# Attention and a top-1 expert layer on one core: score tiles in a ring for the first two quads, and the last quad's sums moved ahead of a group of scores

## The chip, the cores and the metric

The kernel runs on one core of one Trainium2 chip. Times are device microseconds (us) of one execution. The kernel before took 807.14 us in the median of three runs (805.10 to 809.29). TensorE (PE in the profile) multiplies matrices, ScalarE (ACT) evaluates functions, VectorE (DVE) does elementwise work, GpSimd (POOL) issues the gathers, scatters and some copies, and SyncE (SP) issues the loads. PE writes its results to PSUM, a memory of eight banks; a bank holds 512 fp32 numbers for each of the 128 partitions.

## The reference

The inputs are q, k and v of 8 batches, 12 heads, 448 positions and 64 features. The scores are capped with a tanh, and attention is followed by a layer of eight experts of which each token uses one:

```python
scores = q @ k.T / 8
scores = cap * tanh(scores / cap)
attn = exp(scores - max); attn = attn / (sum(attn) + 1e-9)
x = (attn @ v) with the heads side by side        # 3584 tokens x 768
logits = x @ w_gate + modality_bias[modality_id]  # 3584 x 8
e = argmax(logits); gate = softmax(logits)[e]
out = gate * (relu(x @ w1[e]) @ w2[e])            # 768 -> 1024 -> 768
```

## The kernel before

The heads are worked off in 24 **quads**, four heads of one batch each (three quads to a batch). Scores are kept transposed, with keys on partitions and queries along the row, so that the sums over keys are done by PE. The 448 keys of a head are three tiles of 128, and a rest of 64; the rests of the four heads share one tile ("shared", L529 to L537). The two pairs of heads of a quad are t = 0 and t = 1, and the three key tiles are i = 0, 1, 2.

A pass i of the loop at L801 has three parts r, whose operations stand in the list ORDER (L767 to L778), each with the quad that it works on, counted from i. Every engine runs its instructions in the order in which they are issued here. Part 0 makes the shared scores of quad i (`group` with the step None, L563 to L598) and adds the shared products with V of quad i-1 (`pvs`, L617). Part 1 makes the scores of t = 0, then the products with V of t = 1 of quad i-1 (`pv`, L606), copies them out of PSUM (`xs`, L640), and splits the next quad's operands into a rounded and a rest part (`split_hi`, `split_lo`). Part 2 makes the scores of t = 1, then the `sums` of quad i-1 (L648: the softmax denominators and the unscaled gate logits, 16 matmuls in one PSUM tile "glog"), then the products with V of t = 0 of quad i, the copy `gl` of glog (L660), denominators (`den`, L684) and others. In the first pass part 1 comes ahead of part 0, and in the parts (0, 2) and (1, 1) the products with V are issued between the second and the third score tile of the group.

`group` issues the scores of its tiles on PE and then, on ACT, a tanh for each tile and one exponential over all three. A score tile is 128 keys by two heads, two banks of PSUM. There are two pools: `score_tile(4)` gives a tile of four banks, which holds i = 0 and 1 of a group, and `score_tile(2)` gives one of two banks, which holds i = 2 and also the shared scores. In the groups of t = 1 one tanh covers the four banks (L588, L589); in those of t = 0 each tile has its own. The other two banks are xT0 and xT1 (L470 to L472): the accumulators of the products with V, and in between glog and small routing tiles, which take the name in `self.small`.

When a batch's three quads are done, `route` (L238 to L310) works out which expert each token takes and its rank among the expert's tokens: two small matmuls ("rank", L273 and L275), DVE work around them, and four indirect stores to a map in DRAM. It is a generator, of which `next(routing[0])` and STEPS issue a stretch in certain parts. For batch 6 these parts fall in the last pass with scores, i = 23 (= NQ - 1).

In part 2 of pass 23 four operations of the list are replaced (L811, L812): DVE scales the gathered rows of the first expert's tokens, and the turned logits of quad 22 (`lt`, L679) are written to a bank of the score tile. Pass 24 (the list LAST, L779 to L783) ends the last quad and turns the gathered rows on PE (L1054), and the expert stage begins: blocks of 384 tokens, with w1 and w2 of the block's expert loaded, split into two parts and multiplied in three products (L1124, L1125, L1128 and L1160).

Of the kernel before, what the change touches and what calls it, by code (L numbers as in the profile page):

```python
# [39 lines left out]
F32 = mybir.dt.float32  # L40
# [4 lines left out]
ALU = mybir.AluOpType  # L45
AX = mybir.AxisListType
PSUM = bass.MemoryType.PSUM
# [6 lines left out]
KU, KR = 3, 64  # L54
# [26 lines left out]
NQ = NH * B  # L81
# [5 lines left out]
class Program:  # L87
# [8 lines left out]
    def pin(self, inst):  # L96
        return self.tc.keep_in_program_order(inst)
# [365 lines left out]
    def attention(self, first, rp):  # L463
        tc, nc = self.tc, self.nc
        pe, pin = nc.tensor, self.pin
        with ExitStack() as st:
# [3 lines left out]
            ps_x = st.enter_context(tc.tile_pool(name="ps_x", bufs=1, space=PSUM))  # L470
            for t in range(2):
                ps_x.tile([128, 512], F32, name="xT", tag=f"xT{t}")  # L472
            ps_s = [st.enter_context(tc.tile_pool(name=f"ps_s{n}", bufs=1, space=PSUM)) for n in (4, 2)]
            self.ps_r = ps_x
            quads = [dict(live=i < NQ, kq={}, hl={}, pt={}, tot={}, xT={}, xs={}) for i in range(NQ + 1)]

# [46 lines left out]
                        self.scales()  # L523
                quads[0]["hl"][0] = hi, lo

            def score_tile(n):
                return ps_s[n == 2].tile([128, n, 512], F32, name="sc")

            def shared(q):  # L529
                sc = score_tile(2)  # L530
                for t in range(2):
                    for j in range(2):
                        kq, rows = quads[q]["kq"][t], slice(j * D, (j + 1) * D)
                        pin(pe.matmul(
                            sc[t * KR : (t + 1) * KR, j, :S], kq[rows, :KR], kq[rows, KC2:], start=True, stop=True
                        ))
                return sc  # L537

            def scores(q, t, i):
                if i == 0:  # L540
                    quads[q]["four"] = score_tile(4)
                sc = quads[q]["four"][:, 2 * i : 2 * i + 2] if i < 2 else score_tile(2)
                if q == t == i == 0:
                    kq = quads[q]["kq"][t]
                    for j in range(2):
                        rows = slice(j * D, (j + 1) * D)
                        pin(pe.matmul(sc[:, j, :S], kq[rows, KR : KR + 128], kq[rows, KC2:], start=True, stop=True))
                    return sc
                hi, lo = quads[q]["hl"][t]
                ks = slice(i * 128, (i + 1) * 128)  # L550
                for n, (k, x) in enumerate(((hi, hi), (hi, lo), (lo, hi))):
                    for j in range(2):
                        rows = slice(j * D, (j + 1) * D)
                        pin(pe.matmul(sc[:, j, :S], k[rows, ks], x[rows, OWN:], start=n == 0, stop=n == 2))  # L554
                return sc

            def tanh(out, sc, scale):
                pin(nc.scalar.activation(out, sc[:, :, :S], AF.Tanh, scale=scale))  # L558
# [4 lines left out]
            def group(q, steps, amid=None):  # L563

                if q >= NQ:
                    return
                d, made = quads[q], []
                for step in steps:
                    if (q, step) in FILL:
                        self.warm(self.ps_r, FILL[q, step])  # L570
                    if amid and step == steps[-1]:
                        amid()
                    made.append(scores(q, *step) if step else shared(q))
                if "sh" not in d:
                    d["both"] = pp.tile([128, KU + 1, 2, S], F32, name="pt0", bufs=2)
                    d["sh"] = d["both"][:, KU]
                if steps == (None,):
                    tanh(d["sh"], made[0], self.isc)
                    d["later"] = [d["sh"]]
                    if q == 0:  # L580
                        exp(d["later"].pop())
                    return
                t = steps[0][0]
                three = pp.tile([128, KU, 2, S], F32, name="pt1", bufs=1) if t else d["both"]
                scale = 1.0 if (q, t) in SCALED else self.isc
                for n in range(KU):
                    d["pt"][t, n] = three[:, n]
                if t:  # L588
                    tanh(three[:, :2].rearrange("p n j s -> p (n j) s"), d["four"], scale)  # L589
                for n in range(2 if t else 0, KU):  # L590
                    if amid and n == KU - 1 and d.get("later"):
                        exp(d["later"].pop())
                    tanh(three[:, n], made[n], scale)
                whole = three[:, :KU]
                if d.get("later"):
                    d["later"].pop()
                    whole = three
                exp(whole.rearrange("p n j s -> p (n j s)"))  # L598

            FILL = {(0, (1, 2)): 4}  # L600
            SCALED = [(q, t) for q in range(3) for t in range(2)][1:]

# [44 lines left out]

            def sums(q):  # L648
                d = quads[q]
                glog = d["glog"] = ps_x.tile([128, 512], F32, name="glog", tag="xT1" if q < NQ - 1 else "xT0")  # L650
                w = [self.wgt[:, 2 * (q % NH) + t] for t in range(2)]
                for n, four in enumerate((
                    ((0, d["tot"][0][:, 0]), (0, d["tot"][1][:, 0]), (0, d["tot"][0][:, 1]), (2, d["sh"][:, 0])),
                    ((w[0], d["xs"][0]), (w[1], d["xs"][1]), (1, d["tot"][1][:, 1]), (3, d["sh"][:, 1])),
                )):
                    for c, (what, rhs) in enumerate(four):
                        lhs = self.pick[:, what] if isinstance(what, int) else what
                        pin(pe.matmul(glog[c * GW : (c + 1) * GW, :S], lhs, rhs, start=n == 0, stop=n == 1))
# [25 lines left out]
            def den(q):  # L684
                l, gw = quads[q]["lt"], GC if q < NQ - 2 else GW
                b, r = divmod(q, NH)
                if r == 0:
                    lgs[b] = self.lp.tile([CP, C, H, E], F32, name="lg")
                    pays[b] = self.lp.tile([CP, C, MR], F32, name="pay", bufs=2)
                    nc.gpsimd.memset(pays[b][:, :, 2 + H :], 0.0)  # L690
                rec = pays[b][:, :, 2 : 2 + H].rearrange("p c (j k) -> p c j k", j=2)[:, :, :, 2 * r : 2 * r + 2]
                shared = l[:, :, 3 * gw + GE : 3 * gw + GE + 4].rearrange("p c (j t) -> p c j t", j=2)
                pin(nc.vector.tensor_copy(rec, shared))
                for j, own in enumerate((l[:, :, GE : GE + gw + 1 : gw], l[:, :, 2 * gw + GE : 2 * gw + GE + 2])):
                    pin(nc.vector.tensor_tensor(rec[:, :, j], own, rec[:, :, j], op=ALU.add))
                pin(nc.vector.reciprocal(rec, rec))
                for t in range(2):
                    h0 = 4 * r + 2 * t
                    pin(nc.vector.tensor_tensor(
                        lgs[b][:, :, h0 : h0 + 2], l[:, :, t * gw : t * gw + GE].rearrange("p c (j e) -> p c j e", j=2),  # L700
                        rec[:, :, :, t].unsqueeze(3).to_broadcast([CP, C, 2, E]), op=ALU.mult,
                    ))
# [89 lines left out]
            lgs, pays, routing, raws, banks, homes = {}, {}, [], [], [], []  # L792
# [7 lines left out]
            fetch_v(1)  # L800
            for i in range(NQ + 1):  # L801
                for r in (1, 0, 2) if i == 0 else range(3):
                    if (i, r) == (0, 1):
                        split_hi(0, 1)
                        split_lo(0, 1)
                    if (i, r) == (NQ, 0):
                        tot1(NQ - 1, 1)
                        tot2(NQ - 1, 1)
                        self.scale_rows(early[1], homes, (1,))
                    ops = list((ORDER if i < NQ else LAST)[r])  # L810
                    if (i, r) == (NQ - 1, 2):  # L811
                        ops[-4:] = (scale, 0), (lt, -1), (den, -1), ops[-2]  # L812
                    if (i, r) == (NQ - 1, 1):
                        ops.insert(ops.index((split_lo, 1, 0)), (lambda q: next(routing[0]), 0))
                    if (i, r) in ((0, 2), (1, 1)):
                        values = [op for op in ops if op[0] is pv]
                        ops = [op for op in ops if op[0] is not pv]
                        ops[0] += (lambda: [pv(i + n, *how) for _, n, *how in values],)
                    for op, n, *how in ops:
                        q = i + n  # L820
# [4 lines left out]
                    if r == 2:  # L825
                        fetch(i + 2, 1)
                        fetch_v(i + 2)
                    self.small = "xT0" if r == 1 and i else "xT1"
                    for _ in range(STEPS.count((i, r))):
                        next(routing[0], None)  # L830
                    if (i, r) in WAYS:
# [755 lines left out]
```

## Time and profile before

| | |
|---|---|
| median of three runs | 807.14 us (805.10 to 809.29) |
| profiled execution | 803.42 us, span 801.8 us, mean granted clock 0.997 |
| PE busy | 784.8 us (98% of the span), 5184 instructions |
| DVE busy | 556.0 us (69%) |
| ACT busy | 507.3 us (63%) |
| POOL busy | 306.6 us (38%) |

"Busy" is the time in which an engine's instructions run, and for PE the ends of matmuls are modelled. An instruction's idle time is what its engine stood still before it, with what ended that. A line of the profile names the kernel's line, the engine, the operation, and the tiles as out<-in. Attention and its passes reach from the start to about 318 us, and the expert stage from there to the end.

### The profile page before, as it was taken

What the parts mean: (1) busy time and instruction counts of PE and PEld (TensorE: products, weight loads), DVE (VectorE), ACT (ScalarE), POOL (GpSimd) and SP (SyncE); (2) the same over time, 40 slices, a digit from 0 to 9 for tenths busy, and PEclk for the clock granted to TensorE, in tenths of its full rate; (3) what the DMA queues carried; (4) which work ended last, traced back from release to release, by engine and by line L of the source; (5) the groups of instructions that cost most, each with busy time, mean ns of one, the idle gap of its engine ahead of it and who ended that gap; (6) DMA issues with size and microseconds to landing.
All of it is one profiled execution on the core that took longest, in us unless ns stands there. A gap on an engine that the chain in (4) does not pass through costs nothing. (4 is left out here: it accounts for less than half of the span.)

```text
span 801.8 us, 14472 instructions
## 1 busy us (share of the span) xinstructions
PE 784.8 (98%) x5184; PEld 613.9 (77%) x5184; DVE 556.0 (69%) x1085; ACT 507.3 (63%) x552; POOL 306.6 (38%) x382
## 2 busy tenths in 40 slices
PE   7999999999999989999999999999999999999997
PEld 3444544444444444999999999999999999999986
DVE  5889999999999997957284652747527375366820
ACT  7999999999999995256253452534526345245611
POOL 2122434232425162448555173551744407051201
PEclk9999999999999999999999999999999999999999
DMA  7477756767576663498357273563725627257654
GB/s 261 131 180 196 199 134 198 196 159 219 145 216 175 180 165 104 96 315 259 126 183 250 101 239 111 180 237 113 247 103 175 253 93 242 90 176 247 214 216 160
DMA packets 103808, 146.01 MB, mean 182 GB/s; under 512 B 62255, under 2 KB 67457, under 8 KB 103730
## 3 DMA queue, kind: packets, MB, share of 16 engines
q1 hardware_dynamic: 88832, 110.69, 46.2%
q0 software_dynamic: 14752, 34.33, 12.7%
q8 instruction: 43, 0.70, 0.4%
q14 instruction: 35, 0.29, 0.1%
q10 hardware_dynamic: 146, 0.00, 0.0%
HBM read 118.06 MB, written 27.49 MB: 182 GB/s over the span
## 5 line engine op out<-in xcount | busy, mean ns | idle before, releaser
L1124 PE MATMUL ph<-x,ah 128*128 128x384 f32 (+1 forms) x480 | 156.3, 326 | 1.0 <-DVE hl L1135 1.0
L1125 PE MATMUL ph<-x,ah 128*128 128x384 f32 (+1 forms) x480 | 155.9, 325 | 0.0
L1128 PE MATMUL ph<-x,al 128*128 128x384 f32 (+1 forms) x480 | 155.9, 325 | 0.0
L1160 PE MATMUL py<-bh,hh 128*128 128x384 f32 x448 | 150.3, 335 | 0.0
L1160 PE MATMUL py<-bh,hl 128*128 128x384 f32 x448 | 149.8, 334 | 0.0
L1160 PE MATMUL py<-bl,hh 128*128 128x384 f32 x448 | 146.5, 334 | 0.0
L558 ACT ACTIVATE pt<-sc,isc 128x896 f32<-128x896 f32 x132 | 140.2, 1118 | 7.5 <-PE sc L554 4.9
L561 ACT ACTIVATE pt<-pt,cabs 128x2688 f32<-128x2688 f32 (+2 forms) x50 | 140.6, 2811 | 1.6
L991 POOL DMA_INDIRECT xg<-xd,at x93 | 117.8, 1267 | 56.8 <-DVE turned L1077 30.0
L720 POOL DMA_DIRECT2D xd<-xs x96 | 61.1, 644 | 178.2 <-DVE xs L714 175.4
L1012 DVE TENSOR_TENSOR bl<-raw,bh 128x768 fp32r<-128x768 f32 x80 | 74.3, 956 | 70.7 <-ACT bh L1011 70.5
L612 PE MATMUL xT<-pt,va 128*64 128x448 f32 x576 | 118.8, 548 | 0.1
L1134 ACT ACTIVATE hh<-ph 128x384 fp32r<-128x384 f32 (+1 forms) x80 | 37.4, 469 | 126.6 <-PE ph L1128 121.4
L1135 DVE SCALAR_TENSOR_TENSOR hl<-ph,hh 128x384 fp32r<-128x384 f32 (+1 forms) x80 | 41.8, 527 | 105.7 <-ACT hh L1134 105.7
L1124 PEld LDWEIGHTS ph<-x,ah 128*128 128x128 f32 x480 | 90.2, 188 | 1.2 <-DVE hl L1135 1.2
L1125 PEld LDWEIGHTS ph<-x,ah 128*128 128x128 f32 x480 | 90.1, 188 | 0.0
L612 PEld LDWEIGHTS xT<-pt,va 128*64 128x64 f32 x576 | 37.0, 136 | 69.4 <-issue 56.0
L1128 PEld LDWEIGHTS ph<-x,al 128*128 128x128 f32 x480 | 90.1, 188 | 0.0
L1166 POOL DMA_INDIRECT out_dram<-ot,mt x28 | 32.1, 1146 | 146.5 <-ACT ot L1165 128.6
L1160 PEld LDWEIGHTS py<-bh,hh 128*128 128x128 f32 x448 | 84.1, 188 | 1.1 <-issue 0.7
L1160 PEld LDWEIGHTS py<-bh,hl 128*128 128x128 f32 x448 | 84.1, 188 | 0.1
L1160 PEld LDWEIGHTS py<-bl,hh 128*128 128x128 f32 x448 | 83.8, 188 | 0.0
(216 smaller groups left out, 1265.3 us busy)
## 6 DMA issues: line engine op xcount, KB each, us to landing
raw<-in_w_dram SPq DMA_DIRECT2D x86, 384.0 KB, 3.9
raw<-in_w_dram SPq DMA_DIRECT2D x60, 512.0 KB, 5.5
kq<-in_kq_dram SPq DMA_DIRECT2D x47, 448.0 KB, 5.9
va<-in_v_dram SPq DMA_DIRECT2D x24, 448.0 KB, 6.2
xd<-xs POOLq DMA_DIRECT2D x96, 112.0 KB, 5.2
lgd<-gl SPq DMA_DIRECT2D x88, 35.0 KB, 2.9
cg<-lgd SPq DMA_DIRECT2D x22, 140.0 KB, 5.6
raw<-in_w_dram SPq DMA_DIRECT2D x12, 256.0 KB, 5.5
```

Source lines behind the costliest of these rows:

```text
L558: pin(nc.scalar.activation(out, sc[:, :, :S], AF.Tanh, scale=scale))
L561: pin(nc.scalar.activation(x, x, AF.Exp, scale=self.cabs))
L612: pin(pe.matmul(xT[j * D : (j + 1) * D, :S], va[:, u * D : (u + 1) * D], quads[q]["pt"][t, i][:, j], start=t == i == 0, stop=t == 1 and i ...
L720: (nc.gpsimd.dma_start(self.xd[b * S : (b + 1) * S, a, r * 64 : (r + 1) * 64].rearrange("(n p) f -> p n f", p=32), d["out"][a * 32 : (a + ...
L991: got = self.nc.gpsimd.indirect_dma_start(self.xg[:, c], None, self.xd.rearrange("n a x -> (n a) x"), bass.IndirectOffsetOnAxis(ap=at[:, c ...
L1012: b = self.nc.vector.tensor_tensor(lo, raw, hi, op=ALU.subtract)
L1124: nc.tensor.matmul(ph[:, :w], hi[:, fs], self.x[k][:, 0, :w], start=first, stop=False)
L1125: nc.tensor.matmul(ph[:, :w], hi[:, fs], self.x[k][:, 1, :w], start=False, stop=False)
L1128: nc.tensor.matmul(ph[:, :w], lo[:, fs], self.x[k][:, 0, :w], start=False, stop=last)
L1134: nc.scalar.activation(hh[:, f, :w], acc, AF.Relu)
L1135: self.latest["vector"] = nc.vector.scalar_tensor_tensor(hl[:, f, :w], acc, 0.0, hh[:, f, :w], op0=ALU.max, op1=ALU.subtract).ins
L1160: self.latest["tensor"] = nc.tensor.matmul(py[half][:, :HALF], self.h[a][:, f, rows], self.w2s[f][c][:, cs], start=left[half] == 3 * FC - ...
```

## The change

Quads 0 and 1 (RING = 2) take their score tiles from three pools of two banks in turn, and each tile has a tanh of its own. At the start of part 0 of pass 2 the three pools are closed, and a pool of four banks and one of two are opened on the same six banks; from there on the score tiles are as before.

In pass 23 (NQ - 1) the sums and the copy gl of quad 22 are taken out of part 2 and put at the end of part 1, ahead of the second group of scores of quad 23. The routing step that stood in part 1 stays where it was, ahead of them, and the rank step of batch 6 (in STEPS) follows them. glog of quad 22 lies in xT0 now and the small tiles of this part in xT1. The name `eng` in `den` is VectorE, as before.

```diff
-            ps_s = [st.enter_context(tc.tile_pool(name=f"ps_s{n}", bufs=1, space=PSUM)) for n in (4, 2)]
+            ring = ExitStack()
+            score_pool = lambda home, name, **kw: home.enter_context(tc.tile_pool(name=name, bufs=1, space=PSUM, **kw))
+            ps_s = [score_pool(ring, f"ps_s{n}") for n in range(3)]
...
-            def score_tile(n):
+            def score_tile(n=2):
+                if len(ps_s) == 3:
+                    ps_s.append(ps_s.pop(0))
+                    return ps_s[-1].tile([128, n, 512], F32, name="sc")
                 return ps_s[n == 2].tile([128, n, 512], F32, name="sc")
 
+            def pairs():
+                ring.close()
+                ps_s[:] = [score_pool(st, f"ps_s{n}", reuse_waits="tile") for n in ("four", "two")]
...
-                if i == 0:
-                    quads[q]["four"] = score_tile(4)
-                sc = quads[q]["four"][:, 2 * i : 2 * i + 2] if i < 2 else score_tile(2)
+                if i == 0 and q >= RING:
+                    four[:] = [score_tile(4)]
+                sc = four[0][:, 2 * i : 2 * i + 2] if i < 2 and q >= RING else score_tile()
...
-                if t:
-                    tanh(three[:, :2].rearrange("p n j s -> p (n j) s"), d["four"], scale)
-                for n in range(2 if t else 0, KU):
+                joined = t and q >= RING
+                if joined:
+                    tanh(three[:, :2].rearrange("p n j s -> p (n j) s"), four[0], scale)
+                for n in range(2 if joined else 0, KU):
...
+            RING, four = 2, []
...
-                glog = d["glog"] = ps_x.tile([128, 512], F32, name="glog", tag="xT1" if q < NQ - 1 else "xT0")
+                glog = d["glog"] = ps_x.tile([128, 512], F32, name="glog", tag="xT1" if q < NQ - 2 else "xT0")
...
                 for r in (1, 0, 2) if i == 0 else range(3):
+                    if (i, r) == (RING, 0):
+                        pairs()
...
+                    if i == NQ - 1 and r:
+                        late = [(sums, -1), (gl, -1)]
+                        ops = [op for op in ops if op not in late] + (late if r == 1 else [])
...
                     if (i, r) == (NQ - 1, 1):
-                        ops.insert(ops.index((split_lo, 1, 0)), (lambda q: next(routing[0]), 0))
+                        ops.insert(ops.index((sums, -1)), (lambda q: next(routing[0]), 0))
...
-                    self.small = "xT0" if r == 1 and i else "xT1"
+                    self.small = "xT0" if r == 1 and 0 < i < NQ - 1 else "xT1"
```

## Rows read from the trace of the kernel before

**Rows 1.** Table of stretches: us; each engine busy (instructions); PEclk; DMA share; GB/s.

```profile
4.40:12.60 8.20, 5.94 (x42) 3.23 (x42) 6.63 (x20) 6.15 (x5) 0.00 (x0) 1.00 0.97 355
302.70:306.30 3.60, 3.60 (x24) 1.09 (x22) 0.01 (x1) 3.57 (x3) 2.13 (x3) 0.61 0.16 51
304.00:305.00 1.00, 1.00 (x8) 0.20 (x4) 0.00 (x0) 1.00 (x2) 0.69 (x2) 0.50 0.00 0
306.30:317.70 11.40, 9.82 (x67) 4.05 (x65) 11.16 (x32) 4.81 (x8) 2.13 (x2) 1.00 0.34 91
318.10:796.70 478.60, 477.21 (x2926) 472.31 (x2924) 266.81 (x445) 207.66 (x332) 200.66 (x222) 1.00 0.56 185
```

**Rows 2.** ACT in time: start, us, operation, [idle before <-what ended it], quads 0 to 3.

```profile
6.41 2.80 ACT L558 ACTIVATE pt<-sc,isc 128x896 f32<-128x896 f32 x3 [2.24 <-DVE lo L521]
9.25 2.54 ACT L561 ACTIVATE pt<-pt,cabs 128x2688 f32<-128x2688 f32 x1
...
13.67 1.64 ACT L558 ACTIVATE pt<-sc 128x1792 f32<-128x1792 f32 x1
15.89 0.92 ACT L558 ACTIVATE pt<-sc 128x896 f32<-128x896 f32 x1 [0.58 <-PE sc L554]
...
20.17 1.71 ACT L558 ACTIVATE pt<-sc 128x896 f32<-128x896 f32 x2
...
23.26 0.92 ACT L558 ACTIVATE pt<-sc 128x896 f32<-128x896 f32 x1 [0.45 <-PE sc L554]
...
31.59 0.99 ACT L558 ACTIVATE pt<-sc,isc 128x896 f32<-128x896 f32 x1
...
45.09 2.81 ACT L558 ACTIVATE pt<-sc,isc 128x896 f32<-128x896 f32 x3 [0.96 <-PE sc L554]
```

**Rows 3.** PE in order of time, quads 0 to 2.

```profile
9.27 0.59 PE L534 MATMUL sc<-first 64*64 64x448 f32 x2 [2.25 <-ACT pt L558]
...
12.57 2.48 PE L612 MATMUL xT<-pt,va 128*64 128x448 f32 x12
...
29.21 0.98 PE L534 MATMUL sc<-kq 64*64 64x448 f32 x8
...
32.63 0.47 PE L554 MATMUL sc<-hi 64*128 64x448 f32 x2 [0.25 <-ACT pt L558]
```

**Rows 4.** DVE in order of time, the first split of the second load.

```profile
7.33 0.36 DVE L494 CAST hi<-kq 128x384 fp32r<-128x384 f32 x1 [0.92 <-DMA kq<-in_kq_dram]
```

**Rows 5.** PE in order of time, from quad 23 to the expert stage.

```profile
299.57 0.22 PE L273 MATMUL rank<-oh,tri 112*112 112x32 bf16 x1 [1.23 <-DVE oh L260]
300.77 0.18 PE L275 MATMUL rank<-before,ones 112*112 112x32 bf16 x1 [0.98 <-DVE before L265]
...
303.56 0.97 PE L658 MATMUL glog<-tot,pick 128*32 128x448 f32 x3
...
311.66 1.20 PE L1054 MATMUL sc<-ident,pt 128*128 128x128 f32 x9 [1.57 <-DVE lg L699]
...
318.10 0.43 PE L1124 MATMUL ph<-x,ah 128*128 128x384 f32 x1
```

**Rows 6.** PE in order of time, second group and sums of the pass before.

```profile
285.83 0.47 PE L554 MATMUL sc<-hi 64*128 64x448 f32 x2
...
287.85 0.56 PE L658 MATMUL glog<-tot,pick 128*32 128x448 f32 x1
...
289.49 2.48 PE L612 MATMUL xT<-pt,va 128*64 128x448 f32 x12
```

**Rows 7.** DVE in order of time, quad 23.

```profile
297.44 1.08 DVE L638 TENSOR_TENSOR tot<-tot,pt 128x896 f32<-128x896 f32 x1
...
299.44 0.62 DVE L642 COPY xT<-xT 128x448 f32<-128x448 f32 x1
...
300.99 0.19 DVE L279 TENSOR_TENSOR rows<-rank,both 112x32 f32<-112x32 f32 x1
...
306.29 0.62 DVE L664 COPY gl<-glog 128x448 f32<-128x448 f32 x1 [3.60 <-PE glog L658]
```

More of the change, by code (lines that the diff above doesn't have):

```diff
@@ L524, in begin @@
                 quads[0]["hl"][0] = hi, lo
-            def score_tile(n):
+            def score_tile(n=2):
+                if len(ps_s) == 3:
+                    ps_s.append(ps_s.pop(0))
+                    return ps_s[-1].tile([128, n, 512], F32, name="sc")
                 return ps_s[n == 2].tile([128, n, 512], F32, name="sc")
+            def pairs():
+                ring.close()
+                ps_s[:] = [score_pool(st, f"ps_s{n}", reuse_waits="tile") for n in ("four", "two")]
             def shared(q):
-                sc = score_tile(2)
+                sc = score_tile()
                 for t in range(2):
@@ L691, in den @@
                 rec = pays[b][:, :, 2 : 2 + H].rearrange("p c (j k) -> p c j k", j=2)[:, :, :, 2 * r : 2 * r + 2]
+                eng = nc.vector
                 shared = l[:, :, 3 * gw + GE : 3 * gw + GE + 4].rearrange("p c (j t) -> p c j t", j=2)
-                pin(nc.vector.tensor_copy(rec, shared))
+                pin(eng.tensor_copy(rec, shared))
                 for j, own in enumerate((l[:, :, GE : GE + gw + 1 : gw], l[:, :, 2 * gw + GE : 2 * gw + GE + 2])):
-                    pin(nc.vector.tensor_tensor(rec[:, :, j], own, rec[:, :, j], op=ALU.add))
+                    pin(eng.tensor_tensor(rec[:, :, j], own, rec[:, :, j], op=ALU.add))
                 pin(nc.vector.reciprocal(rec, rec))
@@ L698, in den @@
                     h0 = 4 * r + 2 * t
-                    pin(nc.vector.tensor_tensor(
+                    pin(eng.tensor_tensor(
                         lgs[b][:, :, h0 : h0 + 2], l[:, :, t * gw : t * gw + GE].rearrange("p c (j e) -> p c j e", j=2),
```

## The prediction

> **What bounds the kernel now.** I read the page's first two parts first, then the table of stretches, then each engine in order of time where PE or ACT stood still. The page shows PE busy nearly throughout, so a change pays only where it takes idle time from PE's queue, or from an engine on which PE waits there. In the expert stage there is nearly none to take: from the first expert product to the last one PE is busy 477.21 of 478.60 us [rows 1]. Whatever moves the start of that stage should therefore move the end by as much, and the question is when the product at 318.10 starts [rows 5]. Two places decide.
>
> First, quads 0 and 1. ACT starts its first tanh at 6.41 and then works almost without a gap; its gaps are 0.58 us ahead of 15.89 and 0.45 us ahead of 23.26, both times because PE had not finished the scores of the group's third tile [rows 2]. PE in turn had stood for 2.25 us ahead of the shared scores at 9.27, because their score tile was still being read by ACT [rows 3]. So each waits for the other over a single two-bank tile. From the wait at 32.63 (0.25 us for ACT) PE leads: at 45.09 ACT waits 0.96 us for PE [rows 2, 3]. Until about 32 the stage is ACT's, then PE's, and what ACT gains before 32.63 PE inherits.
>
> Second, the last quad. PE stands 1.23 us and 0.98 us around the two rank matmuls [rows 5]; then the granted clock falls to half (0.61 from 302.7 to 306.3, and 0.50 from 304 to 305, the lower of the two levels, 1.2 GHz) [rows 1]; PE gets to the sums of quad 22 only at 303.56 [rows 5]; DVE waits for them for 3.60 us, until 306.29 [rows 7]; and from then on DVE is the chain: it is busy 11.16 of 11.40 us up to 317.7 [rows 1], PE waits for it at 311.66 (1.57 us), and its last scaled rows and subtractions release 318.10 [rows 5]. The 3.60 us are thus on the path.
>
> **The change, part by part.**
>
> *Ring of three in quads 0 and 1.* The shared scores of quad 0 take the tile of the first tanh, free at 6.41 + 2.80/3 = 7.34 [rows 2]. Their keys are there when DVE begins to split the same load, at 7.33 [rows 4]. So they start at about 7.4 instead of 9.27, and the two score groups and the four filling matmuls behind them move up by 1 us or more. Before, PE started the products with V at 12.57 on no wait, though the exponentials were done at 9.25 + 2.54 = 11.79 [rows 2, 3]; now PE is there first, they start at 11.85, take 2.4 and leave 0.65 for the third score group, so its tile is ready at 15.0, ahead of the 15.4 at which ACT has done the two other tanhs. The 0.58 us go. In quad 1 it repeats: PE arrives before the exponential and not after it, and the 0.45 us go; here the margin is only some 0.2 us.
>
> The price is two joined tanhs of 1.64 us that become pairs. The row of two single ones at 20.17 is 1.71 us [rows 2], so 0.07 each, 0.14 together. ACT's tanh of shared scores at 31.59 thus comes 0.58 + 0.45 - 0.14 = 0.89 earlier, and PE's wait at 32.63 ends 0.9 earlier. What is late next there is the same wait. Bounds: -0.14 if neither gap goes, 1.03 if both go and the halves cost nothing. I take 0.9, because both gaps have one cause and the change removes it.
>
> *Change of pools at quad 2.* No row shows one. If each new tile waits only for the readers of its own banks, the tile of two waits for the first tanh of quad 1's second group and the tile of four for the second and third; all three are done about when PE asks, and PE stands at 29.21 behind its own queue anyway [rows 3]: nothing. If the change acts as a barrier up to ACT's last exponential of quad 1, PE loses 2.4 us (priced below). I take nothing, the row at 29.21 being nearest.
>
> *Sums and ranks of quad 22 ahead of the second group.* The products with V of quad 22 end at 299.57 - 1.23 = 298.34 [rows 5]. The first half of the sums needs DVE's total, done at 297.44 + 1.08 = 298.52, and the second half needs the copy of xT, done at 299.44 + 0.62 = 300.06 [rows 7]; DVE's order up to there is unchanged. At full clock the sums take 289.49 - 287.85 = 1.64 [rows 6], so 0.82 a half: first half 298.6 to 299.4, a stall of 0.65, second half 300.1 to 300.95. The ranks' inputs are ready at 300.77 [rows 5], so they cost 0.1 and no wait. The second group's scores start at 301.05 instead of 300.88, 0.17 late; at full clock they take 287.85 - 285.83 = 2.02 [rows 6] and the products with V follow at 303.1. ACT's tanh of them loses nothing, since the clock no longer halves under the second score pair.
>
> On DVE the copy of the logits comes right behind the routing's adds. It waits for the sums until about 301.1, and the rank's rows, which started at 300.99 [rows 7], start at 301.7. The tail that ended at 306.29 - 3.60 = 302.69 ends at 303.4; what followed the copy at 306.29 + 0.54 = 306.83 follows at 303.4. That is 3.4 earlier. Is anything else late? The gathered rows that DVE scales next have landed (no DMA traffic in the stretch from 304 to 305) [rows 1]. The turn of the logits on PE comes after products of 2.48 [rows 3], at 305.6 to 306.2, some 2 us ahead of where 311.66 moves (308.25). DVE has no gap to lose between, so 318.10 becomes 314.7. The cost beside this: the puts of batch 6 to the map go out 0.7 later, on POOL, and nothing reads them before the expert stage. The copy of quad 22's logits issues no DMA, and SP's loads of w1 that wait for the buffers of its totals can only go earlier.
>
> What stays open is the clock. PE's idle time there falls from 2.21 us to about 0.25 + 0.65. If the clock is halved all the same, scores and products come 1.6 us later (the excess worked out below), the turn is done at 307.8 instead of 306.2, DVE needs it at about 307.1, and 0.7 is lost. Bounds 2.7 to 3.4; I take 3.4, since much of the standing still that preceded the fall goes.
>
> **Sum.** The profiled execution is 803.42 (span 801.8 and 1.6 around it). 0.9 + 3.4 = 4.3 gives 799.1. The median of the runs shown, 807.14, is 3.72 above it, and the three reach from 805.10 to 809.29; I put the same difference on top: **802.8**.
>
> **A rule weighed against the trace.** The half clock after PE's waits at 299.57 and 300.77 is in the one profiled execution [rows 1, 5]; the longer single wait ahead of 9.27 had none behind it, the clock being 1.00 from 4.4 to 12.6 [rows 1, 3]. The Trainium skill, "TensorE: Matmul & The Clock Gate", Part 1, says that the window in which activity is judged runs free and does not start with the kernel; by that rule the fall may be missing from some of the timed runs. The trace, being one execution, can't show that. It is the first rival.
>
> **The rivals.**
>
> *The fall of the clock is not typical of the timed runs.* From 300.88 (0.11 behind the second rank) scores and sums took until about 306.2, just ahead of the copy at 306.29 [rows 7], 5.3 us; at full clock they take 289.49 - 285.83 = 3.66 [rows 5, 6]. The excess is 1.6. Without it DVE's wait was only 2.0, and the second part gives 1.8: 807.14 - 2.7 = 804.4. For it: the wait ahead of 9.27 was longer than either of these two and no fall came [rows 1, 3]. Against it: the only execution that is shown has the fall. Chance 0.20.
>
> *The clock falls also early.* Then the wait of 2.25 at 9.27 is followed by a slow stretch in the timed runs, which the ring avoids; at most the same 1.6 more: 801.2. Against it: the clock is 1.00 there in the execution that is shown [rows 1]. Chance 0.08.
>
> *The ring doesn't do what it says.* PE is held in quad 0 or 1 by something that the row hides, and ACT's gaps stay: 3.4 - 0.14, 803.9. Chance 0.11.
>
> *The gain is given back in the expert stage,* if weights or gathers, and not PE, pace it: 807.1. Against it: PE idles 1.4 us in 478.6 [rows 1]. Chance 0.07.
>
> *Slower: the change of pools is a barrier.* At quad 2 PE would stand from 29.21 - 0.9 = 28.3 until ACT's exponentials of quad 1 are done, just ahead of 31.59 - 0.9 = 30.7 [rows 2, 3]: 2.4 us. A wait of that size (2.21 us in two pieces) preceded the fall of the clock [rows 1, 5], so 1.6 more. The start is then 0.9 - 2.4 - 1.6 = -3.1; with the second part at 1.8 the kernel is 1.3 slower, 808.4; with 3.4 it is level. It decides where the second part gives under 3.1. Against it: quad 1's own order needs no barrier. Chance 0.08.
>
> **How the numbers follow.** The forecast has 0.46. A measurement of this kernel tells 0.5%, 4.0 us, from no change; the forecast's 4.3 lies just beyond it, and the runs before spread by 2 us to either side. So faster by over 0.5%: 0.29 of the forecast's 0.46, all of the early fall's 0.08, 0.08 of the two middle rivals: 0.45. Slower by over 0.5%: most of the barrier's 0.08 only if the runs are unlucky as well, and what I overlook: 0.07. The rest, 0.48, is within. The range runs from 799.4 (801.2 less the spread) to 806.9, which takes in the first three rivals and leaves out 0.15 above.
>
> **What would show it.** Right: no ACT wait for PE ahead of the third tanh of either second-quad group; the shared scores of quad 0 at 7.4; quad 2's wait, 32.63, at 31.7; the copy of the logits of quad 22 at about 300.2 (with the 0.9 from the start), the first expert product at 313.8, and no half clock between 301 and 305. Wrong: PE standing over 0.5 us at the shared scores of quad 2; a new DVE wait after the logits' copy; the first expert product later than 316; a longer expert stage than 478.6.

## The result and the profile after

The changed kernel took 796.72 us in the median (796.47 to 797.30, 4 runs) and the kernel before 806.75 (805.10 to 809.29, the three runs shown before and a fourth): 10.0 us less between the medians, ratio 0.989 [0.9853, 0.9926], which is 8.9 us. The forecast was 802.8 with a range down to 799.4. The direction was right and the size was more than double the 4.3 us forecast.

The profiled execution took 796.47 (span 794.9), 6.95 less than the profiled one of before. So two things are to be explained: where those 6.95 went, and why the medians differ by 3 more: the changed kernel's median is 0.25 above its profiled execution, that of before 3.33.

The table of stretches of the kernel after (us; busy of PE, PEld, DVE, ACT, POOL; PEclk; DMA share; GB/s). The second stretch is where the last pass's sums and ranks now stand, the third is DVE's chain to the expert stage, the last is the expert stage:

```profile
4.40:12.60 8.20, 7.65 (x46) 3.68 (x48) 6.47 (x20) 6.52 (x6) 0.00 (x0) 1.00 0.97 355
297.10:300.70 3.60, 3.46 (x28) 1.56 (x28) 3.10 (x15) 2.68 (x2) 2.73 (x4) 1.00 0.88 284
300.80:312.20 11.40, 10.85 (x77) 4.78 (x73) 11.09 (x35) 8.42 (x10) 7.11 (x4) 1.00 0.39 124
312.60:789.10 476.50, 476.50 (x2926) 472.48 (x2924) 266.84 (x445) 207.73 (x332) 200.55 (x222) 1.00 0.56 186
```

Beside [rows 1]: PE's 5.94 us of work in the first stretch are 7.65, the half clock of 302.7 to 306.3 is gone, and the expert stage is 476.5 long instead of 478.6, with no idle PE at all.

ACT of the kernel after in order of time, quads 0 to 2 (line numbers are those of the changed file: L567 is the tanh, L563 and L543 the scores, L623 the products with V, L669 the sums):

```profile
6.01 2.81 ACT L567 ACTIVATE pt<-sc,isc 128x896 f32<-128x896 f32 x3 [1.87 <-DVE isc L185]
...
13.27 2.51 ACT L567 ACTIVATE pt<-sc 128x896 f32<-128x896 f32 x3
...
21.72 0.92 ACT L567 ACTIVATE pt<-sc 128x896 f32<-128x896 f32 x1
...
30.11 0.99 ACT L567 ACTIVATE pt<-sc,isc 128x896 f32<-128x896 f32 x1
```

Both gaps of [rows 2] are gone, as forecast. What was not forecast is the first line: the first tanh starts at 6.01 instead of 6.41. ACT's tanh of quad 2 comes 1.48 earlier (30.11 against 31.59), 0.4 of it from there. PE of the kernel after, same stretch:

```profile
7.08 0.59 PE L543 MATMUL sc<-first 64*64 64x448 f32 x2
...
11.49 2.48 PE L623 MATMUL xT<-pt,va 128*64 128x448 f32 x12
...
18.40 2.48 PE L623 MATMUL xT<-pt,va 128*64 128x448 f32 x12 [0.55 <-ACT pt L570]
...
27.67 0.98 PE L543 MATMUL sc<-kq 64*64 64x448 f32 x8
...
31.15 0.47 PE L563 MATMUL sc<-hi 64*128 64x448 f32 x2 [0.32 <-ACT pt L567]
```

The 2.25 us ahead of the shared scores are gone; PE waits at 18.40 for the exponential instead, as forecast. Quad 2 starts at 27.67 instead of 29.21 [rows 3], 1.54 earlier, and the change of pools costs nothing there.

PE and then DVE of the kernel after in the last pass:

```profile
297.50 1.62 PE L669 MATMUL glog<-xT,wgt 128*32 128x448 f32 x3
...
299.43 0.22 PE L273 MATMUL rank<-oh,tri 112*112 112x32 bf16 x1
299.51 0.20 PE L275 MATMUL rank<-before,ones 112*112 112x32 bf16 x1
...
301.69 2.48 PE L623 MATMUL xT<-pt,va 128*64 128x448 f32 x12
...
306.20 1.20 PE L1071 MATMUL sc<-ident,pt 128*128 128x128 f32 x9 [0.55 <-DVE lg L711]
...
312.64 0.42 PE L1141 MATMUL ph<-x,ah 128*128 128x384 f32 x1
```

```profile
297.88 0.61 DVE L653 COPY xT<-xT 128x448 f32<-128x448 f32 x1
...
299.59 0.62 DVE L675 COPY gl<-glog 128x448 f32<-128x448 f32 x1 [0.22 <-PE glog L669]
300.13 0.18 DVE L279 TENSOR_TENSOR rows<-rank,both 112x32 f32<-112x32 f32 x1
...
301.38 1.06 DVE L645 TENSOR_TENSOR tot<-pt 128x896 f32<-128x896 f32 x1
```

DVE's wait of 3.60 for the sums is 0.22 [rows 7]. The first expert product stands at 312.64 instead of 318.10 [rows 5]: 5.46, of which 1.54 come from the start and 3.92 from the last pass. The expert stage gives 2.1 more in this pair, and the work behind its last product takes 0.65 longer (5.1 and 5.8 us up to the end of the span), which makes the 6.95.

### The profile page after: what moved, and what is told of

It reads as the page before. It is cut to its first block, busy times and chain, and to the rows that moved or that the text cites. A ratio compares the mean times of both kernels' runs of the same rounds, so it can differ in the third digit from the quotient of the medians.

```text
span 794.9 us, 14474 instructions
## 1 busy us (share of the span) xinstructions
PE 783.8 (99%) x5184; PEld 613.6 (77%) x5184; DVE 556.0 (70%) x1085; ACT 507.1 (64%) x554; POOL 310.1 (39%) x382
## 5 line engine op out<-in xcount | busy, mean ns | idle before, releaser
L567 ACT ACTIVATE pt<-sc,isc 128x896 f32<-128x896 f32 x132 | 140.2, 1118 | 7.3 <-PE sc L563 5.2
L1008 POOL DMA_INDIRECT xg<-xd,at x93 | 115.5, 1242 | 55.6 <-DVE turned L1094 28.8
L623 PE MATMUL xT<-pt,va 128*64 128x448 f32 x576 | 118.8, 548 | 0.6 <-ACT pt L570 0.5
L623 PEld LDWEIGHTS xT<-pt,va 128*64 128x64 f32 x576 | 37.0, 136 | 69.4 <-issue 56.2
```

Source lines behind the costliest of these rows:

```text
L623: pin(pe.matmul(xT[j * D : (j + 1) * D, :S], va[:, u * D : (u + 1) * D], quads[q]["pt"][t, i][:, j], start=t == i == 0, stop=t == 1 and i ...
L1008: got = self.nc.gpsimd.indirect_dma_start(self.xg[:, c], None, self.xd.rearrange("n a x -> (n a) x"), bass.IndirectOffsetOnAxis(ap=at[:, c ...
```

## The experiments

Each row compares with runs of the kernel before on the same chip. There were three chips, with four rows each; the medians of before there were 807.75, 804.90 and 806.57. "Clock" is the mean of the runs' granted clocks. A "fall" is a stretch in which the granted clock is 0.50, the lower of its two levels. "Idle matmuls" are matmuls whose result nobody reads, put where PE would stand still.

| kernel | median us | clock | ratio to before [95%] |
|---|---|---|---|
| before, again | 807.82 | 0.9936 | 1.0005 [0.9975, 1.0036] |
| ring alone | 803.43 | 0.9958 | 0.9971 [0.9944, 0.9997] |
| sums' move alone | 804.49 | 0.9951 | 0.9962 [0.9936, 0.9989] |
| both, as changed | 797.53 | 0.9981 | 0.9902 [0.9866, 0.9938] |
| before, idle matmuls at the start | 804.73 | 0.9970 | 0.9997 [0.9968, 1.0027] |
| before, idle matmuls at both places | 803.76 | 0.9984 | 0.9980 [0.9952, 1.0008] |
| before, first tiles swapped | 803.88 | 0.9968 | 0.9959 [0.9928, 0.9990] |
| changed, ring to quad 22 | 796.54 | 0.9982 | 0.9891 [0.9857, 0.9925] |
| ring, idle matmuls in the last pass | 800.74 | 0.9982 | 0.9936 [0.9911, 0.9962] |
| sums' move, idle matmuls at the start | 800.23 | 0.9985 | 0.9931 [0.9904, 0.9958] |
| both, as changed, third chip | 798.36 | 0.9984 | 0.9905 [0.9869, 0.9941] |
| changed, ring to quad 22, again | 795.46 | 0.9990 | 0.9873 [0.9838, 0.9909] |

**The kernel before, once more.** No edit.

> The kernel before, once more, as a control beside the others. Theory A (the change moves the first expert product 5.5 us earlier, and the rest of the 10.0 us between the medians is how the weights' loads of those runs fell in time): a new profile of it has the first expert product at 318.1 within 0.5 us, with the half clock after the rank matmuls, but other waits in the expert stage than 0.35 and 1.04 us, and its timed runs differ from one another by 1 us or more, in the expert stage's part alone. Theory B (the runs of before lose time regularly that the profile shown does not show, such as a second fall of the clock): the new profile or the granted clocks of the timed runs show more half clock than the first, 0.995 or less.

Its runs had a mean clock of 0.994, where the profile shown had 0.997; its first expert product came at 320.55, and its new profile has a second fall, behind the wait of quad 0 (us; PE busy; PEclk; DMA share; GB/s):

```profile
9.00:10.00 1.00, 0.04 (x4) 1.00 1.08 379
10.00:11.00 1.00, 1.00 (x8) 0.54 0.96 384
11.00:12.00 1.00, 1.00 (x6) 0.50 1.07 434
12.00:13.00 1.00, 1.00 (x8) 0.50 1.02 416
...
304.00:305.00 1.00, 1.00 (x8) 0.50 0.86 338
```

In order of time, PE and then ACT of that execution:

```profile
9.96 0.93 PE L534 MATMUL sc<-first 64*64 64x448 f32 x2 [2.29 <-ACT pt L558]
...
31.48 0.98 PE L534 MATMUL sc<-kq 64*64 64x448 f32 x8
```

```profile
7.10 2.80 ACT L558 ACTIVATE pt<-sc,isc 128x896 f32<-128x896 f32 x3 [3.01 <-PE sc L554]
...
18.16 0.92 ACT L558 ACTIVATE pt<-sc 128x896 f32<-128x896 f32 x1 [2.16 <-PE sc L554]
```

The gap ahead of the third tanh is 2.16 instead of 0.58, and from the first tanh to quad 2 it is 24.38 instead of 22.80: this fall costs 1.58 us, right where PE and ACT wait for each other. Theory A had no such fall and fails on that; theory B's point is shown. Over 96 runs of before, the time goes with the granted clock (correlation -0.86): the 11 with 0.991 or less have a median of 810.75, the 42 at 0.994 and 0.995 have 805.67, the 9 at 0.998 or more have 802.22.

**Each part alone, and both again.** The two parts of the diff, separated.

> Only the ring of three in quads 0 and 1. Theory A: the first expert product 1.5 us earlier than before (first tanh 0.4 earlier, as it no longer waits for the second key tile; the gaps of 0.58 and 0.45 us gone; 0.1 back for the split tanhs), and the time lower by 1.5 us. Theory B: more than 3 us, because the waits of quad 0 no longer bring the clock down in the timed runs.

> Only the last quad's sums and ranks ahead of its second group. Theory A: the first expert product 3.9 us earlier than before, no half clock between 299 and 306, the time lower by 3.9 us if the expert stage stays as long as it was, and by up to 6 if its waits at 360 and 766 are also gone. Theory B: 7 us or more, the expert stage's waits being a consequence of where its start falls.

> Both parts, the changed kernel again. Theory A: the sum of the two parts, 5.4 us at the first expert product, and a difference to the kernel before of 5.5 to 7.5 us on the same chip. Theory B: 10 us again, with runs as close together as 0.8 us.

Each part gives 2 to 3 us and both give 7.9 by the ratio, though the intervals are wide. The time settles none of the theories: the ring's 2.3 lies between 1.5 and 3, the move's 3.1 is under 3.9, and the 7.9 of both is just above 7.5, with runs from 796.68 to 803.57. In the profile of the ring alone the first fall is missing and the waits around the ranks remain. In the profile of the sums' move the fall of quad 0 is there (quad 2 at 31.07) and the last pass has none. With the ring alone a fall came at another place in its profile, behind PE's wait ahead of the turn of the gathered rows:

```profile
308.77 2.16 PE L1068 MATMUL sc<-ident,pt 128*128 128x128 f32 x9 [1.77 <-DVE lg L711]
```

That matmul group took 1.20 at full clock [rows 5]; this wait is 0.55 in the changed kernel. So there are three waits of PE behind which the profiles show a fall: in quad 0, at the ranks, and at the turn. Each part alone leaves at least one of them. None of them brings a fall every time: the waits at the ranks stand in five executions (before, its copy, the ring alone, and two kernels below), and a fall came right behind them in the first two only.

**Idle matmuls in the waits, with the order of before.** Two kernels: one with the first edit, one with both.

```diff
-            FILL = {(0, (1, 2)): 4}
+            FILL = {(0, None): 10, (0, (1, 2)): 4, (1, None): 4}
...
+                    if (i, r) == (NQ - 1, 1):
+                        self.warm(self.ps_r, 10)
```

> The kernel before with idle matmuls in PE's waits ahead of the shared scores of quad 0 (10) and quad 1 (4); order, tiles and everything else as before. Theory A (a wait of PE, not the order itself, brings the clock down in some executions, and a fall costs about 2 us): the granted clock never falls before 250 us, the mean clock of the timed runs rises from 0.994 to about 0.996, and the median is 1.5 to 2.5 us lower than before, though no real work starts earlier than in a run of before without a fall. Theory B (the clock only goes along with something else that is slow, such as the loads): the median stays within 1 us of before, whatever the clock.

> As the one with idle matmuls in quads 0 and 1, and 10 more ahead of the rank matmuls of the last pass. Theory A: mean clock of the timed runs 0.998, as with both parts of the change; median 802.5 (the level that the runs of before reach without a fall), so about 5 us below before and 4 to 5 us above the changed kernel, which has the order as well. Theory B: within 1.5 us of before.

The clock did what was expected: 0.9970 and 0.9984, and no fall in either profile. In the first kernel the waits at the ranks are still there (1.22 and 0.98), so that its profile has none is partly chance. With the falls gone the sums of the last pass are where the prediction's first rival had them, DVE's wait 2.2 and the copy at 304.85 (304.65 there); PE and DVE of the second kernel:

```profile
298.18 2.33 PE L192 MATMUL idle<-ones 112*128 112x512 bf16 x10
300.57 0.18 PE L273 MATMUL rank<-oh,tri 112*112 112x32 bf16 x1
```

```profile
304.85 0.62 DVE L664 COPY gl<-glog 128x448 f32<-128x448 f32 x1 [2.22 <-PE glog L658]
```

```profile
316.67 0.42 PE L1126 MATMUL ph<-x,ah 128*128 128x384 f32 x1
```

The last line is its first expert product. Its quad 2 starts at 29.23, as in the kernel before (29.21), so the fall in the last pass cost 318.10 - 316.67 = 1.43. The times fell by less than expected: 1.6 us by the ratio, with an interval from 3.9 faster to 0.6 slower, and nothing measurable with the start alone. On before alone the price of the falls is thus shown by the traces, but not by the timed runs. The expectation of 5 us had read the price of a fall from how time and clock go together over the runs, which is too much.

**The same on each part alone.** The same edits, on the ring alone (last pass) and on the sums' move alone (start).

> The ring alone, with 10 idle matmuls ahead of the rank matmuls of the last pass, so that both places of PE's waiting are covered. Theory A (a fall of the clock costs 1.6 us and before has about two in a run; the order of the ring alone is worth 1.5 us): mean clock 0.998, 4.5 us below before (3.0 to 6.0), and the first expert product at 315.0 in a profile without a fall. Theory B (the falls cost nothing that the order doesn't cost as well): no lower than the ring without idle matmuls, 2.3 us below before.

> The sums' move alone, with idle matmuls in PE's waits of quads 0 and 1. Theory A: mean clock 0.998, 5.3 us below before (3.5 to 7.0): 2.3 of the order when no fall stands in the last pass, and 3.0 of two falls; first expert product at 314.3. Theory B: no lower than the move without idle matmuls, 3.1 us below before.

> The changed kernel on the same chip as these. Theory A (parts add once falls are counted apart): 6.8 us below before, between 5.5 and 9, and about 2 us below each of the two with idle matmuls. If it is 9 or more again, and 4 or more below them, something beside the order and the clock is in it.

The ring goes from 0.9971 to 0.9936 and the move from 0.9962 to 0.9931, 2.5 to 3 us each, with a clock of 0.998 in both. Against before that is 5.2 and 5.6 us, as theory A has it in both; but the intervals of with and without overlap, and the two were on different chips, so this step is not shown by itself. The ring's profile has a fall all the same, at the turn, and its first expert product is at 316.80 and not at the 315.0 expected:

```profile
309.03 2.13 PE L1070 MATMUL sc<-ident,pt 128*128 128x128 f32 x9 [1.76 <-DVE lg L711]
```

Both parts are again some 2 us below either one (798.36 against 800.74 and 800.23), with no interval taken between them.

**Which part of the first tile the first tanh waits for.**

```diff
-                if i == 0:
+                n = (i - 1) % KU if q == t == 0 else i
+                if n == 0:
                     quads[q]["four"] = score_tile(4)
-                sc = quads[q]["four"][:, 2 * i : 2 * i + 2] if i < 2 else score_tile(2)
+                sc = quads[q]["four"][:, 2 * n : 2 * n + 2] if n < 2 else score_tile(2)
```

> The kernel before, with one difference: in the very first group the first key tile's scores go into the tile of two banks, and the second and third into the tile of four. Theory A (a tanh that reads half of the four-bank tile waits until PE has written the other half too): the first tanh starts 0.4 us earlier, at 6.0; the shared scores of quad 0 follow at 7.5, as with the ring, since they wait for the first tanh only; no fall of the clock at 10; about 1 us earlier at quad 2 than a run of before without a fall. Theory B (the first tanh waits for the scale, which DVE makes): the first tanh at 6.4 as before.

```profile
6.19 1.01 ACT L559 ACTIVATE pt<-sc,isc 128x896 f32<-128x896 f32 x1 [2.08 <-PE sc L548]
7.64 1.91 ACT L559 ACTIVATE pt<-sc,isc 128x896 f32<-128x896 f32 x2 [0.44 <-PE sc L555]
```

The first tanh now waits for its own scores (L548) alone, and the second, which reads half of the four-bank tile, starts only when the third tile's scores are written, at 7.64. In the copy of before above, the first tanh waited for L554, the second tile's matmuls, until 7.10. So in this program a tanh of half the tile does wait for the other half. The row shown before named DVE for that wait [rows 2], a coincidence of ends. The shared scores started at 7.53, as expected, and no fall came at 10, but one did later, at 310.31, behind the wait of 1.77 at the turn. Quad 2 came at 28.86, only 0.35 earlier than in the profile of before and not 1: the gap of quad 1 stayed, 0.44. The time is 0.4% lower.

**The ring kept longer.**

```diff
-            RING, four = 2, []
+            RING, four = NQ - 1, []
```

> The changed kernel with the ring of three kept up to quad 22 instead of quad 1, so without joined tanhs there. If a tanh of half the four-bank tile waits for the other half in every quad, and PE leads, the ring gives up to 0.3 us in a quad where ACT waits; against it stand 0.07 us of ACT for each of the 21 more split tanhs, 1.5 us in all. Theory A: within 1.5 us of the changed kernel, to either side, quads a little longer where ACT is the bound. Rival: 3 us or more faster, the joined tile having been the limit of the whole attention stage.

> The ring kept up to quad 22, beside the changed kernel on the same chip: the first profile had its first expert product 1.5 us earlier than the changed kernel's. If that is of the order and not of that run: 1 to 2 us below the changed kernel. If it is not: the same within 0.8 us.

Waits of ACT between 32 and 290 us, the changed kernel and then this one (us in total, times, longest):

```profile
ACT pt L567 <- PE sc L563: 3.8, 9, 1.0
```

```profile
ACT pt L567 <- PE sc L563: 0.3, 1, 0.3
```

```profile
311.33 0.42 PE L1141 MATMUL ph<-x,ah 128*128 128x384 f32 x1
```

The last line is its first expert product, 1.3 us ahead of the changed kernel's, and on the same chip its median is 2.9 below it, where 1 to 2 were expected. Its ratio to before is 0.9873 [0.9838, 0.9909]. No interval against the changed kernel was taken, but its six runs lie at 794.72 to 797.27 and the seven of that one at 797.09 to 804.17; in this kernel's two profiles the first expert product came 1.3 and 1.5 us earlier than in the first of the changed kernel. The rival's 3 us in the order itself are not there.

## Why the prediction was wrong

*Two places decide; the expert stage passes the gain on.* Right: 312.64 for 318.10, and a stage that is no longer than before.

*Ring of three, 0.9.* The mechanism was right step by step (shared scores at 7.08 for 7.4, both ACT gaps gone, the wait at 18.40, split tanhs at no more than the price named). The term was 1.54. Most of the missing part is the wait of the first tanh for the other half of its tile, 0.40, which the row put down to DVE. From the first tanh to ACT's tanh of quad 2 the gain is 1.08 (24.10 for 25.18) and not 0.89, as the split tanhs cost next to nothing of the 0.14 put down for them.

*Change of pools, nothing.* Right; the barrier rival fell, PE standing nowhere at 27.67.

*Sums and ranks, 3.4.* Right in order and near in size, 3.92. The copy came at 299.59 for about 300.2, with no stall worth naming ahead of the second half. Of the rest, 0.39 is a wait in the routing's tail behind the rank, which stood in the kernel before:

```profile
302.02 0.17 DVE L287 CAST pos<-posf 112x4 int32<-112x4 f32 x1 [0.39 <-DVE posf L285]
```

It is in the kernel with idle matmuls at both places too, and gone in the changed one; its cause is not shown. Of the 3.92, 1.43 is the fall of the clock that the profiled execution of before happened to have there. Without it the order gives 2.5, where the rival said 1.8.

*The sum: "I put the same difference on top".* This is the step that failed. The 3.72 by which the median of before lay above its profiled execution was carried over whole to the changed kernel, where it measured 0.25. The difference between the two is 3.5 of the 6.1 us between 802.8 and 796.72. (The other 2.6 are 1.2 by which the two terms were too small, and 1.5 of the expert stage and what follows it, which no term forecast.) The sum took the gain of one execution of before, which had one fall of the clock, and carried it to runs that had, by the mean clocks, about two more than the changed kernel's. A fall lowers the mean clock by about 0.002 (0.997 with one, 0.999 with none in the two profiles), the runs of before stand at 0.994, those after at 0.998.

The rival "the clock falls also early" was the case in the copy of before, and had a chance of 0.08; its price of at most 1.6 was right for one fall. The likelier rival of the opposite sign, that the fall in the last pass is not typical, is half true: behind the ranks it came in two executions of five, but two of the other three had it at the turn, and a mean clock of 0.994 leaves no room for runs mostly without falls. That a fall may be missing from some runs cuts both ways: the prediction weighed the missing of a seen fall more than the presence of an unseen one, though the 2.25 us wait ahead of 9.27 was the longest of all.

Put together at full clock the order is worth 1.5 + (3.9 - 1.4) = 4.0 us; two falls fewer are worth about 3. That makes 7, inside the interval of 6.0 to 11.9, for the 10.0 of the medians; the three ratios of the changed kernel say 8.9, 7.9 and 7.7. The rest is not settled. The 2.1 us of the expert stage are not the change's: the copy of before had that stage at 476.5, as after, and in 13 of the 14 profiles, whatever the kernel, it lies between 476.3 and 478.7. The start may be some of it: the profiled execution of before had the earliest first tanh of six (6.41, the median being 6.96), and the changed kernel's three lie at 6.01 to 6.19, so about 0.4 us (an estimate from these). The timed runs agree in part. At a clock of 0.998 or more the nine runs of before have a median of 802.22 and the fifteen of the changed kernel, in its three groups, 797.30: 4.9 us less, beside the 4.0 of the traces. The other 5 us of the medians go along with the clock; that falls alone make them is not shown.

## What to carry to other kernels

A wait of TensorE can cost more than its length, because the clock may fall behind it. Here falls came behind waits of 1.8 to 2.3 us, in some executions and not in others, and one cost 1.4 to 1.6 us. So look at the mean granted clock of the timed runs before one profile is taken for all, and don't carry the distance between a profile and the median over to a kernel that has fewer such waits. A tile that two producers fill in halves and whose halves are read apart is better made two tiles: here the reader of the first half waited for the second. And where a chain engine stands still for a result that PE has queued behind other work, moving that work ahead can gain the wait even if PE itself gains little: here 3.60 us of waiting became 0.22.

## What was not expected of the hardware

PE's first score matmuls took longer than later ones, up to a time that differed between executions. The same operation took 0.58 us at 6.69 in the kernel of before with idle matmuls at the start, and 0.37 from 5.57 on in the changed kernel; the third line is of the recorded fall in the copy of before:

```profile
6.69 0.58 PE L554 MATMUL sc<-hi,lo 64*128 64x448 f32 x2
```

```profile
5.57 0.37 PE L563 MATMUL sc<-lo,hi 64*128 64x448 f32 x2
```

```profile
12.49 0.58 PE L554 MATMUL sc<-hi,lo 64*128 64x448 f32 x2
```

The clock column shows 1.00 throughout the first two, but that is no measurement: the traces' first record of the clock is at 7.44 in the one and at 4.78 in the other, just where the matmuls become faster, and 0.58 is what the operation takes at a recorded clock of 0.50. So PE evidently starts at the lower level, and when it leaves it differs from execution to execution. In the kernel before the first record is at 5.10, so the 1.00 that the prediction read from 4.4 on holds only from there. The first tanh came at 6.41 to 7.31 in six executions of kernels with the four-bank tile, where it waits for the scores of two tiles, and at 6.01 to 6.20 in seven with the ring, where it waits for those of one.

And PE can stand for its own instructions: in one execution of the changed kernel (802.6 us of span, 7.7 more than the profile after) matmuls of the expert stage waited about 4.1 us in all with no releaser shown, and the clock fell there once; that stage was 7.5 us longer. The first of these waits:

```profile
375.94 0.34 PE L1141 MATMUL ph<-x,ah 128*128 128x384 f32 x1 [0.93 <-issue]
```

What holds PE there is not shown. This is the run of 804.17 us at a clock of 0.997; whether others of the slowest runs are of this kind is not shown either.
